# Summing v over each partition's keys before the expert guess, and a new order of GpSimd's work in batches 0 and 1

## The chip, the cores and the metric

The kernel runs on one core of one Trainium2 chip. The metric is the device time of one execution in microseconds (us). Five engines of the core work side by side, each through its own instruction list in order: TensorE (PE in the profile; PEld is its weight load), VectorE (DVE), ScalarE (ACT), GpSimd (POOL) and SyncE (SP, which here only issues transfers). They wait for each other through semaphores. Transfers are issued by SP, ACT or POOL and run on 16 shared DMA engines.

## What is computed

Grouped-query attention, then a mixture of experts, for 8 batches of 384 tokens:

```python
B, Hq, S, D = 8, 16, 384, 64          # 4 key/value heads, 4 query heads each
scores = q @ k.T / sqrt(D)            # softmax over the keys, per head
attn   = exp(scores) / sum(exp(scores))
x      = (attn @ v) as (B*S, 1024)    # all heads of a token side by side
g_idx  = argmax(x @ w_group)          # one of 4 groups, per token
e_idx  = argmax(x @ w_expert[g_idx])  # one of 4 experts of that group
h      = relu(x @ w1[g_idx, e_idx])   # 1024 x 1024
out    = p_group * p_expert * (h @ w2[g_idx, e_idx])
```

p_group and p_expert are the softmax weights of the choices. The scores are small, so attn @ v is close to the mean of v over the keys. With these inputs all 384 tokens of a batch choose the same expert.

## The kernel before, in words

**Batches and units.** The attention of a batch is cut into 24 units u: 4 key/value heads (groups g = u // 6) of 6 pieces of 64 keys. `Attn.run` does for each unit, two units ahead, the scores (L310, TensorE) and their exp (L316, ScalarE, into a tile `e` of a ring of 13), then the products with v (`pv`, L329), then `tail`: GpSimd adds pairs of `e` tiles (L336, emitted at pieces 1 and 3), VectorE reduces four tiles of each group over the partitions' 32-blocks (L343). After a group the sums of products are copied out of PSUM into `xT` (L379 VectorE or L381 ScalarE).

**Softmax sums.** `collect` (L405) adds a group's four reductions on VectorE, `sums` (L415, TensorE, then a reciprocal, L419) finishes them, `spread` (L426, VectorE) spreads the reciprocals over the lanes and `scale_x` (L435) multiplies `xT` by them; `normalise` is the last two on VectorE. `cast` (L244, L246) writes the bf16 copy `xb` that the experts read.

**Guess and fetch.** The weights of one expert are 4 MB. They are fetched before the tokens' own choice is known, for a guessed expert: `guess_mean` (L461) sums v over the keys on TensorE, with slices of v as the stationary side and a column of ones as the moving side (12 products of one column for a batch), `mean_copy` brings the result to SBUF, `guess_logits` (L474) multiplies it by the gate matrix `wgd` (4 products), VectorE picks the largest logit (`first_pick`, `gate_softmax`, `pick_index`), and GpSimd reads the index (`pick`) and issues the fetches of w1 (`pick_w1`, L545) and w2 (`pick_w2`, L551). Ahead of them GpSimd runs a tiny copy (`transposed`, L674) that waits until the next batch's q has been transposed, so that the fetch does not run beside DMA transposes. Experts that were not guessed right are done by a loop at the end (L892); its count is found at run time.

**Order of the work.** All instruction orders are written out by hand (`manual_schedule`). `run` takes a table from unit to inserted steps. Batch 0 (L713) and the first 16 units of batch 1 (L734) hold the first guess, the first fetches, the normalising of batch 0 and the loads of batch 2. Reductions of batch 1 are held back and let go together at unit 11 (`release`). The experts' first product of batch 0, `moe_h(0, 0)` (L607), follows unit 15. From batch 2 on, `block(b)` follows the attention of batch b: `prefetch`, then the experts' products of batch b-1 (`moe_h` L607, `moe_y` L618, output L643/L645/L647) with the softmax sums, the gate logits (L451) and the guess of batch b+1 between them. Batch 7 has no next batch, so its block has no guess. At the end the experts of batch 7 run alone (L879), their outputs are scaled on ScalarE (L884) and VectorE (L882) in turn, and leave by transfers issued on SP, the very last half on ACT (L887).

The start (`first_scores`) casts and transposes the first k and q on TensorE, with `fill` products of ones between, which keep TensorE busy while data arrive.

Of the kernel before, what the change touches and what calls it, by code (L numbers as in the profile page):

```python
# [9 lines left out]
F32 = mybir.dt.float32  # L10
BF16 = mybir.dt.bfloat16
I32 = mybir.dt.int32
AX = mybir.AxisListType
ALU = mybir.AluOpType
# [4 lines left out]
def kernel(  # L19
# [11 lines left out]
    nc = tc.nc  # L31
    P = 128
# [158 lines left out]
    half32 = cpool.tile([P, 2, H2], F32)  # L191
    nc.vector.memset(half32, 0.0)
    wgs = gpool.tile([P, Hkv, NW], F32, name="wgs")
    wgd = cpool.tile([P, Hkv, NW], BF16)
    eidx = cpool.tile([P, NE], F32)
    eback = cpool.tile([P, NE], F32)
    pidx = cpool.tile([P, 3, B, NE], F32)
# [36 lines left out]
    def gate_matrix_b():  # L234
        p2 = ps_tile("x")[:, 1, :Hkv * NW].rearrange("p (g n) -> p g n", n=NW)
        nc.tensor.matmul(out=p2, lhsT=mod64.rearrange("p a m -> p (a m)"), rhs=wgs,
                         start=True, stop=True)
        nc.vector.tensor_copy(out=wgd, in_=p2)

    def evac(eng, out_, in_):
        if eng is nc.scalar:
            eng.copy(out=out_, in_=in_)  # L244
        else:
            eng.tensor_copy(out=out_, in_=in_)  # L246
# [18 lines left out]
    def first_scores():  # L265
        new_kT(0)
        new_qT(0)
        warm = ps_tile("o")

        def fill(n):  # L270
            for i in range(n):
                nc.tensor.matmul(out=warm[:, i % 2, :], lhsT=onesb[:, :P], rhs=onesb, start=True,
                                 stop=True)

        for i in range(4):
            nc.tensor.matmul(out=warm[:, i % 2, :P], lhsT=ones1, rhs=ones1, start=True, stop=True)
        fill(6)
        nc.vector.tensor_copy(out=k16[0][:, :NC].rearrange("p c d -> p (c d)"), in_=k0f[:, 0])
        nc.scalar.copy(out=qraw[0][:, 0], in_=q0f[:, 0])
        nc.vector.tensor_copy(out=qraw[0][:, 1], in_=q0f[:, 1])  # L280
        first_k(0, "s", nc.scalar)
        first_q(0, SC, "s", nc.vector)
        fill(1)
        first_q(SC, SC, "o", nc.vector)
        fill(2)

# [7 lines left out]
    class Attn:  # L294
# [62 lines left out]
        def tail(self, u):  # L357
            b = self.b
            g, c = u // NC, u % NC
            z = u - c  # L360
            if c in (1, 3):
                self.add(nc.gpsimd, u - 1)
            if (b, g) == (2, 0):
                for n in ((), (1,), (2, 0))[max(c, 3) - 3]:
                    self.reduce(g, n, (z, z + 4, z + 5)[n])
            elif c >= 3:
                self.reduce(g, c - 3, (z, z + 4, z + 5)[c - 3])
            if c == NC - 1:
                self.reduce(g, NR - 1, z + 2)
                if b not in xT:  # L370
                    if b == 1:
                        w = wpool.tile([P, KQ, F], BF16, name="w1")
                        xT[b] = w.rearrange("p a f -> p (a f)").bitcast(F32)[
                            :, :KQ * S].rearrange("p (a n) -> p a n", n=S)
                    else:
                        xT[b] = xpool.tile([P, KQ, S], F32, name="xT", bufs=1)
                dst, src = xT[b][:, KG * g:KG * (g + 1), :], self.oT[g][:, :, :S]
                if b > 1 and g < Hkv - 1 or (b, g) == (1, 1):
                    nc.vector.tensor_copy(out=dst, in_=src)  # L379
                else:  # L380
                    nc.scalar.copy(out=dst, in_=src)  # L381
# [64 lines left out]
    def gate_logits(b, pt):  # L446

        for kq in range(KQ):
            x = xT[b][:, kq, :].rearrange("p (c t i) -> p t c i", t=4, i=32)
            for t in range(4):  # L450
                nc.tensor.matmul(out=pt[32 * t:32 * t + 32, 0, :32 * SC], lhsT=wg[:, kq, :],  # L451
                                 rhs=x[:, t], start=(kq == 0), stop=(kq == KQ - 1))

    def guess_mean(b, pt):

        pm = pt[:, 1, :Hkv]
        v16 = vraw[b].rearrange("p h x -> p (h x)").bitcast(BF16)
        for g in range(Hkv):
            for i in range(SC):
                e0 = g * NC * D + i * P  # L460
                nc.tensor.matmul(out=pm[:, g:g + 1], lhsT=v16[:, 2 * e0 + 1:2 * (e0 + P):2],  # L461
                                 rhs=onesb[:, :1], start=(i == 0), stop=(i == SC - 1))

    def mean_copy(pt, eng):
        vm = gpool.tile([P, Hkv], BF16, name="vm")
        evac(eng, vm, pt[:, 1, :Hkv])
        return vm

    def guess_row(pt):
        return pt[:, 1, 64:64 + NW]  # L470

    def guess_logits(vm, pt):
        for g in range(Hkv):
            nc.tensor.matmul(out=guess_row(pt), lhsT=vm[:, g:g + 1].to_broadcast([P, P]),  # L474
                             rhs=wgd[:, g, :], start=(g == 0), stop=(g == Hkv - 1))

    def gate_softmax(b, pt, guess):

# [104 lines left out]
    def out_weights(b):  # L583
        m = gpool.tile([P, SC, NE], F32, name="m")
        nc.vector.tensor_tensor(out=m, in0=cw_all[:, b],
                                in1=oh1_all[:, b, :].unsqueeze(1).to_broadcast([P, SC, NE]),
                                op=ALU.mult)
        we = gpool.tile([P, SC], F32, name="we", bufs=2)
        nc.vector.tensor_reduce(out=we, in_=m, axis=AX.X, op=ALU.add)
        weff[b] = we  # L590
# [43 lines left out]
    def moe_h(b, f0, which, mid=None):  # L634
        if f0 == 0:
            hTs[b] = xpool.tile([P, FQ, S], BF16, name="hT", bufs=1)
        ffn_h(xb[b], w1s[b], hTs[b], f0, which, mid)
# [14 lines left out]
    def do(f, *a):  # L652
        return lambda: f(*a)
# [54 lines left out]
    def first_spread():  # L708
        state["rb"] = spread(0, 1)

    GB = KG * SC
    a = at[0]
    a.run(0, NU, {  # L713
        1: [do(first_q, GB, GB, "x", nc.vector)],
        3: [cast_k],
        4: [gate_matrix_b],
        6: [do(collect, 0, 0, 1)],
        7: [do(first_q, 2 * GB, 2 * GB, "x", nc.vector)],
        8: [do(first_k, 1, "x", nc.vector)],
# [1 line left out]
        13: [first_guess],  # L721
        14: [do(cast, 0, 0)],
        15: [do(collect, 0, 1, 2), first_pick],
        16: [first_fetch],
        19: [do(sums, 0, 1, 2, "x")],
        20: [first_spread],
        21: [first_scale],
    }, at[1])
# [3 lines left out]
    a = at[1]  # L732
    hold(a)
    a.run(0, FU, {  # L734
        3: [do(pick_w2, 0)],
        4: [do(sums, 0, 2, Hkv, "x")],
        6: [do(normalise, 0, 2, "x"), do(normalise, 0, 3, "x")],
        9: [do(load_k, 2), do(load_q, 2)],
        10: [do(cast, 0, 2)],
        11: [a.release, do(collect, 1, 0, 2)],  # L740
        13: [do(cast, 0, 3)],
    })
    moe_h(0, 0, "s")
    load_v(2, nc.gpsimd)
# [10 lines left out]
    weights[0] = gate_softmax(0, pt, True)  # L755
    pick_index(1)
    moe_h(0, 6, "s")
    a.run(FU, NU, {})

    def first_block():  # L760

# [39 lines left out]
    def block(b):  # L801
        last = b == B - 1
        f = b - 1
        if not last:
            prefetch(b)
        moe_h(f, 0, "s")
        collect(b, 0, Hkv)
        weights[f]()
        out_weights(f)
        moe_h(f, 2, "s")  # L810
        sums(b, 0, Hkv, "o")
        for m in range(4):
            normalise(b, m)
        moe_h(f, 4, "s")
        moe_h(f, 6, "s")
        cast(b, 0)
        cast(b, 1)
        moe_y(f, 0, "s")
        cast(b, 2)
        cast(b, 3)  # L820
        y = ffn_y(w2s[f], hTs[f], 1, "s", (0,))
        pt = ps_tile("o")
        gate_logits(b, pt)
        if not last:
            guess_mean(b + 1, pt)
            vm = mean_copy(pt, nc.vector)
        ffn_y(w2s[f], hTs[f], 1, "s", (1,), y)
        y_out(f, 1, y)
        if not last:
            guess_logits(vm, pt)  # L830
        weights[b] = gate_softmax(b, pt, not last)
        y = ffn_y(w2s[f], hTs[f], 2, "o", (0,))
        if not last:
            pick_index(b + 1)
            at[b + 1] = Attn(b + 1)
            y_scores(f, at[b + 1], y)
            return {}
        ffn_y(w2s[f], hTs[f], 2, "o", (1,), y)
        y_out(f, 2, y, nc.vector)
        weights[b]()  # L840
        out_weights(b)
# [28 lines left out]
    for c in range(SC):  # L870
        ot = opool.tile([P, DM], F32, name="ot")
        w = weff[B - 1][:, c:c + 1]
        parts = [(0, HALF), (HALF, DM)]
        if c == SC - 1:
            parts = [(0, HALF), (HALF, 3 * HALF // 2), (3 * HALF // 2, DM)]
        for i, (n0, n1) in enumerate(parts):
            y = ps_tile("so"[i % 2])
            for f in range(FQ):
                nc.tensor.matmul(out=y[:, 0, :n1 - n0], lhsT=hTs[B - 1][:, f, c * P:(c + 1) * P],  # L879
                                 rhs=w2s[B - 1][:, f, n0:n1], start=(f == 0), stop=(f == FQ - 1))  # L880
            if i % 2:
                nc.vector.tensor_scalar(ot[:, n0:n1], y[:, 0, :n1 - n0], w, None, op0=ALU.mult)  # L882
            else:
                nc.scalar.mul(ot[:, n0:n1], y[:, 0, :n1 - n0], w)  # L884
            for j, (ps, x) in enumerate(halves(c)):
                eng = nc.scalar if j and n1 - n0 < HALF and i == 2 else nc.sync
                eng.dma_start(out=out_rows(out[(B - 1) * S:])[x][:, n0:n1], in_=ot[ps, n0:n1])  # L887
    region.close()

# [84 lines left out]
```

## Time and profile before

| | us |
|---|---|
| four runs | 367.66 to 369.09, median 367.97 |
| the profiled execution | 367.97 |
| its span, first to last instruction | 366.3 |
| end of its last matmul | 359.3 |
| TensorE / VectorE / ScalarE / GpSimd busy | 354.5 / 258.9 / 229.0 / 152.2 |
| attention of batch 3, units 0 to 23 | 124.0 to 143.1 |
| experts' block between two attentions | 100.0 to 124.0 |
| after the last attention | 315.3 to 366.3 |

The profiled execution's own time equals the median of the runs; 1.6 us of it lie outside its span. "Busy" counts an instruction from its start to its end; matmuls overlap each other, so a busy TensorE can still have its instructions further apart or closer together. The chain of waits follows the execution back from its last instruction, at each step to what released it. A line number names the line of the kernel; where a helper records an operation it is the helper's.

### The profile page before, as it was taken

The page shows a single profiled execution, that of the slowest core. Times are in us where ns is not written, and L with a number is a line of the kernel's source. Part 1 is how long each engine was busy: PE and PEld are TensorE (multiplying, and loading weights), DVE is VectorE, ACT ScalarE, POOL GpSimd, SP SyncE. Part 2 cuts the span into 40 slices and gives each one's busy share as a digit, 9 for nine tenths or more (in the row PEclk, how much of TensorE's full clock was granted, in tenths as well). Part 3 has the DMA queues.
Part 4 walks back from the last instruction along what each step waited for, and adds up shares of the span by engine and source line. Part 5 has one row for each costly group of instructions (what it writes and reads, how often), then busy time and mean ns, then how long its engine had stood idle before and what let it go on. Part 6 is the DMA issues. An engine that isn't in the chain of part 4 may idle for free.

```text
span 366.3 us, 9583 instructions
## 1 busy us (share of the span) xinstructions
PE 354.5 (97%) x3989; PEld 185.8 (51%) x4004; DVE 258.9 (71%) x500; ACT 229.0 (63%) x300; POOL 152.2 (42%) x120
## 2 busy tenths in 40 slices
PE   8999899999999999999999999999999999999992
PEld 4554465455455445554455555554555545555641
DVE  5698799759975698837878479755997459892130
ACT  5799835659835796348944498356963579444221
POOL 6756960517704375035732177042760258300000
PEclk9999999999999999999999999999999999999998
DMA  8976999899999999899999999999997699997234
GB/s 189 252 115 105 192 207 197 177 229 244 209 138 196 257 238 207 143 215 268 222 152 185 196 265 210 143 205 240 240 208 128 96 272 229 214 212 179 70 86 92
DMA packets 69903, 69.81 MB, mean 191 GB/s; under 512 B 35832, under 2 KB 49944, under 8 KB 69856
## 3 DMA queue, kind: packets, MB, share of 16 engines
q0 software_dynamic: 26864, 41.81, 65.0%
q1 hardware_dynamic: 42560, 26.80, 31.9%
q8 instruction: 33, 0.54, 0.6%
q10 hardware_dynamic: 432, 0.54, 0.5%
q14 instruction: 14, 0.11, 0.1%
HBM read 89.21 MB, written 12.58 MB: 278 GB/s over the span
## 4 chain that ended last, share of the span: by engine, by line
PE 90%; DVE 3%; ACT 2%; DMA 1%; issue 1%; POOL 1%; ACTq 0%
PE ps_o L329 30%; PE ps_s L607 22%; PE ps_s L618 13%; PE ps_s L310 8%; PE ps_o L618 7%; PE ps_o L451 3%; PE ps_s L879 2%; DVE red L343 1%; PE ps_o L607 1%; PE ps_o L879 1%; ACT e L316 1%; PE ps_o L415 1%; DMA w<-in_q_dram 1%; PE ps_o L461 1%; DVE ps_o L426 1%
## 5 line engine op out<-in xcount | busy, mean ns | idle before, releaser
L316 ACT ACTIVATE e<-ps_s 128x768 f32<-128x768 f32 x192 | 150.1, 815 | 19.2 <-PE ps_s L310 16.5
L329 PE MATMUL ps_o<-e,v_raw 64*64 64x384 f32 x1536 | 153.1, 482 | 0.2 <-DVE xT L435 0.2
L336 POOL TENSOR_TENSOR e<-e 128x768 f32<-128x768 f32 x64 | 116.0, 1831 | 80.1 <-ACT e L316 59.3
L343 DVE TRANSPOSE_TENSOR_REDUCE red<-e 128x24 f32<-128x768 f32 x128 | 114.1, 946 | 18.4 <-POOL e L336 18.3
L607 PE MATMUL ps_s<-xb,w 128*128 128x384 bf16 x480 | 81.0, 326 | 0.1
L329 PEld LDWEIGHTS ps_o<-e,v_raw 64*64 64x64 f32 x1536 | 55.6, 133 | 37.4 <-issue 27.0
L607 PEld LDWEIGHTS <-w 128*128 128x128 bf16 x512 | 48.9, 98 | 35.8 <-issue 4.2
L310 PE MATMUL ps_s<-qT,kT 64*64 64x384 bf16 x768 | 63.7, 326 | 0.5 <-ACT e L316 0.2
L611 ACT ACTIVATE hT<-ps_s 128x768 bf16<-128x768 f32 x30 | 24.3, 811 | 61.0 <-PE ps_s L607 61.0
L618 PE MATMUL ps_s<-w,hT 128*128 128x512 bf16 x211 | 49.0, 379 | 0.9 <-issue 0.2
L618 PEld LDWEIGHTS <-hT 128*128 128x128 bf16 x336 | 31.3, 98 | 36.6 <-issue 2.1
L310 PEld LDWEIGHTS <-kT 64*64 64x64 bf16 x768 | 24.5, 105 | 38.4 <-issue 36.5
L643 ACT ACTIVATE ot<-ps_s,we 128x1024 f32<-128x1024 f32 x14 | 15.6, 1115 | 27.3 <-PE ps_s L618 27.3
L674 POOL COPY after<-qT 128x1 bf16<-128x1 bf16 x7 | 2.4, 344 | 69.7 <-DMA qT<-q_raw 66.0
L426 DVE STREAM_TRANSPOSE rb<-inv 128x384 f32<-128x384 f32 x60 | 31.0, 554 | 0.3
L618 PE MATMUL ps_o<-w,hT 128*128 128x512 bf16 x111 | 26.3, 379 | 0.1
L435 DVE TENSOR_TENSOR xT<-xT,rb 128x768 f32<-128x768 f32 x25 | 24.0, 958 | 0.9
L244 ACT CAST xb<-xT 128x768 bf16<-128x768 f32 x27 | 21.1, 828 | 0.0
L379 DVE COPY xT<-ps_o 128x768 f32<-128x768 f32 x18 | 16.5, 919 | 0.0
L246 DVE CAST vm<-ps_o 128x4 bf16<-128x4 f32 x6 | 1.0, 162 | 21.0 <-PE ps_o L461 21.0
L645 DVE TENSOR_SCALAR ot<-ps_o,we 128x1024 f32<-128x1024 f32 x7 | 9.0, 1282 | 5.6 <-PE ps_o L618 5.1
L545 POOL DMA_DIRECT2D w<-in_moe_w_dram x8 | 7.3, 915 | 12.4 <-PE ps_s L310 9.7
(125 smaller groups left out, 197.2 us busy)
## 6 DMA issues: line engine op xcount, KB each, us to landing
w<-in_moe_w_dram POOLq DMA_DIRECT2D x16, 2048.0 KB, 23.2
out_dram<-ot SPq DMA_DIRECT2D x42, 256.0 KB, 6.8
q_raw<-in_q_dram POOLq DMA_DIRECT2D x7, 768.0 KB, 31.4
v_raw<-in_v_dram SPq DMA_DIRECT2D x12, 384.0 KB, 5.5
k<-in_k_dram POOLq DMA_DIRECT2D x7, 192.0 KB, 28.1
out_dram<-ot SPq DMA_DIRECT2D x10, 128.0 KB, 2.3
v_raw<-in_v_dram POOLq DMA_DIRECT2D x2, 384.0 KB, 12.2
w<-in_q_dram POOLq DMA_DIRECT2D x3, 192.0 KB, 6.7
```

The costliest lines, as they stand in the source:

```text
L244: eng.copy(out=out_, in_=in_)
L310: nc.tensor.matmul(out=sT[r * H2:(r + 1) * H2, s, :S], lhsT=kT[b][s * D:(s + 1) * D, slot, ks], rhs=qT[b][s * D:(s + 1) * D, kq * SC:(kq + ...
L316: nc.scalar.activation(e.rearrange("p t (s x) -> p s t x", s=2), sT[:, :, :S].rearrange("p s (t x) -> p s t x", t=2), ACT.Exp, scale=scale)
L329: nc.tensor.matmul(out=oT[t * D:(t + 1) * D, r, :S], lhsT=vraw[b][r * H2:(r + 1) * H2, g, c * D:(c + 1) * D], rhs=self.e[u][r * H2:(r + 1) ...
L336: eng.tensor_add(out=self.e[u], in0=self.e[u], in1=self.e[u + 1])
L343: nc.vector.tensor_reduce(out=reds[self.b][:, g, n].rearrange("p t j -> p (t j)"), in_=self.e[u].rearrange("p t (j x) -> p (t j) x", x=32) ...
L379: nc.vector.tensor_copy(out=dst, in_=src)
L426: nc.vector.transpose(out=rb[:, r].rearrange("p (j x) -> p j x", x=32), in_=inv[b][:, 2 * m + r].unsqueeze(2).to_broadcast([P, NB, 32]))
L435: eng.tensor_mul(out=x, in0=x, in1=rb)
L607: nc.tensor.matmul(out=h[:, jj, :S], lhsT=w1[:, kq, (f0 + jj) * P:(f0 + jj + 1) * P], rhs=x[:, kq, :], start=(kq == 0), stop=(kq == KQ - 1))
L611: nc.scalar.activation(hT[:, f0:f0 + 2, :], h[:, :, :S], ACT.Relu)
L618: nc.tensor.matmul(out=y[:, nh, :], lhsT=hT[:, f, c * P:(c + 1) * P], rhs=w2[:, f, nh * HALF:(nh + 1) * HALF], start=(f == 0), stop=(f == ...
```

## The change

1. **The sum of v.** A new step `sum_v` adds, on every partition, the 6 keys that lie there, for 4 heads of 64 columns (1536 numbers to 256, fp32 in, bf16 out). For batches 1 and 3 to 7 it is one VectorE reduce; for batches 0 and 2 it is three adds on GpSimd (768, 256 and 256 wide). `guess_mean` then needs 2 products of one column instead of 12, with two heads side by side, and `guess_logits` 2 instead of 4; `wgd` is laid out for two heads side by side, which takes two copies of half the partitions instead of one.
2. **Where `sum_v` stands.** Batch 0: GpSimd, after unit 4 of batch 0, behind `cast_k`. Batch 1: VectorE, after unit 5 of batch 1. Batch 2: GpSimd, after unit 21 of batch 1. Batches 3 to 7: VectorE, in the block before, between `out_weights` and the second `moe_h`.
3. **First fetch.** `first_fetch` moves from unit 16 to unit 19 of batch 0, so GpSimd's add of unit 19 stands ahead of it.
4. **Group 2 of batch 0** is scaled on GpSimd (`second_scale`, after unit 5 of batch 1) and no longer on VectorE after unit 6; the add of unit 3 of batch 1 and the fetch of w2 (unit 3 before) stand right behind it. The casts of groups 2 and 3 move from units 10 and 13 to units 9 and 11.
5. **Start and end.** One `fill` product between the first transposes goes. In the last outputs the second half of every part that ScalarE scales is issued by ACT, not by SP: three transfers more on ACT, three fewer on SP.

```diff
-    wgd = cpool.tile([P, Hkv, NW], BF16)
+    wgd = cpool.tile([P, Hkv // 2, NW], BF16)
...
-        nc.vector.tensor_copy(out=wgd, in_=p2)
+        for r in range(2):
+            nc.vector.tensor_copy(out=wgd[r * H2:(r + 1) * H2], in_=p2[r * H2:(r + 1) * H2, r::2])
...
         first_q(0, SC, "s", nc.vector)
-        fill(1)
         first_q(SC, SC, "o", nc.vector)
...
-            if c in (1, 3):
+            if c in (1, 3) and (b, u) != (1, 3):
                 self.add(nc.gpsimd, u - 1)
...
+    def sum_v(b, eng):
+        vsum[b] = gpool.tile([P, Hkv, D], BF16, name="vsum")
+        with nc.allow_low_precision("only serves a guess"):
+            if eng is nc.vector:
+                eng.tensor_reduce(out=vsum[b], in_=vraw[b].rearrange("p g (c d) -> p g d c", d=D),
+                                  axis=AX.X, op=ALU.add)
+                return
+            n = NC // 2 * D
+            t = gpool.tile([P, 2, S], F32, name="rb", bufs=2).rearrange(
+                "p a s -> p (a s)").rearrange("p (g n) -> p g n", g=Hkv)
+            eng.tensor_add(out=t, in0=vraw[b][:, :, :n], in1=vraw[b][:, :, n:])
+            eng.tensor_add(out=t[:, :, :D], in0=t[:, :, :D], in1=t[:, :, D:2 * D])
+            eng.tensor_add(out=vsum[b], in0=t[:, :, :D], in1=t[:, :, 2 * D:])
...
     def guess_mean(b, pt):
-        pm = pt[:, 1, :Hkv]
-        v16 = vraw[b].rearrange("p h x -> p (h x)").bitcast(BF16)
-        for g in range(Hkv):
-            for i in range(SC):
-                e0 = g * NC * D + i * P
-                nc.tensor.matmul(out=pm[:, g:g + 1], lhsT=v16[:, 2 * e0 + 1:2 * (e0 + P):2],
-                                 rhs=onesb[:, :1], start=(i == 0), stop=(i == SC - 1))
+        for j in range(Hkv // 2):
+            nc.tensor.matmul(out=pt[:, 1, j:j + 1],
+                             lhsT=vsum[b][:, 2 * j:2 * j + 2, :].rearrange("p g d -> p (g d)"),
+                             rhs=onesb[:, :1], start=True, stop=True)
...
     def guess_logits(vm, pt):
-        for g in range(Hkv):
-            nc.tensor.matmul(out=guess_row(pt), lhsT=vm[:, g:g + 1].to_broadcast([P, P]),
-                             rhs=wgd[:, g, :], start=(g == 0), stop=(g == Hkv - 1))
+        n = Hkv // 2
+        for j in range(n):
+            nc.tensor.matmul(out=guess_row(pt), lhsT=vm[:, j:j + 1].to_broadcast([P, P]),
+                             rhs=wgd[:, j, :], start=(j == 0), stop=(j == n - 1))
...
+    def second_scale():
+        scale_x(0, 2, spread(0, 2), nc.gpsimd)
...
-        4: [gate_matrix_b],
+        4: [gate_matrix_b, do(sum_v, 0, nc.gpsimd)],
...
-        16: [first_fetch],
-        19: [do(sums, 0, 1, 2, "x")],
+        19: [first_fetch, do(sums, 0, 1, 2, "x")],
...
-        3: [do(pick_w2, 0)],
         4: [do(sums, 0, 2, Hkv, "x")],
-        6: [do(normalise, 0, 2, "x"), do(normalise, 0, 3, "x")],
-        9: [do(load_k, 2), do(load_q, 2)],
-        10: [do(cast, 0, 2)],
-        11: [a.release, do(collect, 1, 0, 2)],
-        13: [do(cast, 0, 3)],
+        5: [second_scale, do(a.add, nc.gpsimd, 2), do(pick_w2, 0), do(sum_v, 1, nc.vector)],
+        6: [do(normalise, 0, 3, "x")],
+        9: [do(load_k, 2), do(load_q, 2), do(cast, 0, 2)],
+        11: [a.release, do(collect, 1, 0, 2), do(cast, 0, 3)],
...
-    a.run(FU, NU, {})
+    a.run(FU, NU, {21: [do(sum_v, 2, nc.gpsimd)]})
...
         out_weights(f)
+        if not last:
+            sum_v(b + 1, nc.vector)
         moe_h(f, 2, "s")
...
-                eng = nc.scalar if j and n1 - n0 < HALF and i == 2 else nc.sync
+                eng = nc.scalar if j and i % 2 == 0 else nc.sync
```

More of the change, by code (lines that the diff above doesn't have):

```diff
@@ L452, in gate_logits @@
                                  rhs=x[:, t], start=(kq == 0), stop=(kq == KQ - 1))
-    def guess_mean(b, pt):
-        pm = pt[:, 1, :Hkv]
-        v16 = vraw[b].rearrange("p h x -> p (h x)").bitcast(BF16)
-        for g in range(Hkv):
-            for i in range(SC):
-                e0 = g * NC * D + i * P
-                nc.tensor.matmul(out=pm[:, g:g + 1], lhsT=v16[:, 2 * e0 + 1:2 * (e0 + P):2],
-                                 rhs=onesb[:, :1], start=(i == 0), stop=(i == SC - 1))
+    vsum = {}
+    def sum_v(b, eng):
[11 more added lines that the diff above has]
+            eng.tensor_add(out=vsum[b], in0=t[:, :, :D], in1=t[:, :, 2 * D:])
+    def guess_mean(b, pt):
+        for j in range(Hkv // 2):
+            nc.tensor.matmul(out=pt[:, 1, j:j + 1],
+                             lhsT=vsum[b][:, 2 * j:2 * j + 2, :].rearrange("p g d -> p (g d)"),
+                             rhs=onesb[:, :1], start=True, stop=True)
     def mean_copy(pt, eng):
-        vm = gpool.tile([P, Hkv], BF16, name="vm")
-        evac(eng, vm, pt[:, 1, :Hkv])
+        vm = gpool.tile([P, Hkv // 2], BF16, name="vm")
+        evac(eng, vm, pt[:, 1, :Hkv // 2])
         return vm
```

## The prediction

> **What bounds the kernel.** I read the first line of the page first.
>
> ```profile
> PE 354.5 (97%) x3989; PEld 185.8 (51%) x4004; DVE 258.9 (71%) x500; ACT 229.0 (63%) x300; POOL 152.2 (42%) x120
> ```
>
> TensorE is busy for 97% of the span, so an edit counts where it takes work from TensorE, or where TensorE waits. The clock granted to it is full until 362 us, so no stage runs slower than another for that reason. The chain of waits then shows where the edited steps lie. Here it is in the block of batch 3 (start, length, what; xN counts instructions):
>
> ```profile
> 116.25 1.46 PE ps_o L451 x64
> 117.70 0.39 PE ps_o L461 x12
> 118.09 0.08 issue
> 118.17 1.67 PE ps_s L618 x7
> 119.84 0.09 PE ps_o L474 x4
> ```
>
> The guess (L461, L474) stands between other TensorE work, nothing else is waited for, and the end is set through it. The same stretch of batch 7, which has no guess, goes straight from L451 to L618:
>
> ```profile
> 331.45 1.46 PE ps_o L451 x64
> 332.91 0.16 issue
> 333.07 1.67 PE ps_s L618 x7
> ```
>
> From L451's end to L618 it is 0.47 us with the guess and 0.16 without. In batches 0 and 1 the chain leaves TensorE:
>
> ```profile
> 31.40 1.83 POOL e L336
> ...
> 33.26 3.57 DVE red L343 x4
> ...
> 36.85 0.49 DVE rsum L405
> ...
> 37.38 0.42 PE ps_o L415 x8
> ...
> 46.81 0.82 ACT e L316
> ...
> 47.67 2.76 PE ps_s L607 x16
> ```
>
> GpSimd's last add of batch 0 stands behind the first fetch; VectorE, the softmax sums, ScalarE's exps and the first experts' product follow from it.
>
> **1. Guess products: -2.1 us.** In the trace the weight loads of L461 start 0.025 us apart, and so do those of L474. Ten pairs fewer (12 to 2) and two fewer (4 to 2) make 12 x 0.025 = 0.30 us per batch, which agrees with the 0.31 just read. Eight guesses: those of batch 1 (51.9), batch 2 (78) and batches 3 to 7 (blocks as above) lie on the chain: 7 x 0.30 = 2.1. Batch 0's (22.65, 24.78) lies in a stretch where ScalarE works without a break from 20.5 to 36.5 and the next thing waited for is VectorE at 37.38; I count it 0 (ends 0 and 0.3).
>
> The Trainium skill, "TensorE: Matmul & The Clock Gate", section "Back-to-back issue gap", gives about 81 ns for a sustained pair of load and product at 128 columns, and some 25 ns as the issue floor for narrow ones. By the first figure, 84 pairs would be worth an estimated 6.8 us; the trace shows 25 ns with a one-column moving side and 128-column weights, and the trace decides.
>
> **2. VectorE's reduce: 0, if it is short enough.** No row shows a reduce with a 256-byte stride. The nearest:
>
> ```profile
> L405 DVE TENSOR_REDUCE rsum<-red 128x96 f32<-128x384 f32 x6 | 4.8, 807 | 0.2
> L866 DVE TENSOR_REDUCE left<-pkey 128x1 f32<-128x128 f32 x1 | 0.3, 288 | 0.0
> L497 DVE TENSOR_REDUCE el<-pr 128x16 f32<-128x64 f32 x7 | 1.9, 266 | 0.2
> L525 DVE TENSOR_REDUCE fmx<-ps_o 128x1 f32<-128x4 f32 x1 | 0.2, 155 | 0.0
> ```
>
> With 0.15 us fixed (L525, 4 elements), L866 gives (288-150)/128 = 1.08 ns per element in order and L405, whose four addends lie apart, (807-150)/384 = 1.71. For 1536 elements that is 1.8 to 2.8 us. I take 2.8, since L405 too reads apart. In a block it stands behind these:
>
> ```profile
> 104.88 0.20 DVE L589 TENSOR_REDUCE we<-m 128x3 f32<-128x48 f32 x1
> 105.81 0.76 DVE L419 RECIPROCAL inv<-ps_o 128x96 f32<-128x96 f32 x1 [0.72 <-PE ps_o L415]
> ...
> 113.49 0.96 DVE L435 TENSOR_TENSOR xT<-xT,rb 128x768 f32<-128x768 f32 x1
> 118.13 0.16 DVE L246 CAST vm<-ps_o 128x4 bf16<-128x4 f32 x1 [3.68 <-PE ps_o L461]
> ```
>
> The 0.72 us idle ahead of L419 takes its start; the other 2.1 are queued in front of L419, the transposes (L426) and the scalings (L435), whose last then ends at 114.45 + 2.1 = 116.5. Its readers: the last quarter of L451, from 117.15 on, and ScalarE's casts of xb, up to 0.2 us late, with no ScalarE work due until 119.9. So it costs nothing; VectorE's 3.68 us of idle pay. With a reduce of over about 3.4 us the cover is gone, and each further us costs one in each of five blocks.
>
> **3. The stretch of batches 0 and 1: -0.1 us.** GpSimd, step by step. Its three adds of v follow `cast_k` (ends 13.70): 768 wide, 1.83 by the rows of L336; 256 wide, a third, some 0.65 each; so they end near 16.95. The adds of units 7 and 9 (15.06 and 17.57 before) then end at 18.8 and 20.6, and VectorE's reduction that stands at 18.54 starts near 18.85; about 0.4 us of that (ends 0 and 0.9) passes through VectorE to `spread(0, 1)`, which ends at 32.3 instead of 31.9. The add of unit 19 has its operands at 27.4 and now stands ahead of the fetch:
>
> ```profile
> 29.82 0.19 POOL L674 COPY after<-qT 128x1 bf16<-128x1 bf16 x1 [3.74 <-DVE red L343]
> 30.45 0.93 POOL L545 DMA_DIRECT2D w<-in_moe_w_dram  x1 [0.44 <-issue]
> ```
>
> It fits into the 3.74 us idle (done 29.3). The wait that the tiny copy makes ends at 29.8 as before, so the fetch of w1 is not moved (it lands 13.9 us later at 44.4, needed at 47.6). VectorE no longer waits 1.36 us for GpSimd: four reductions 32.3 to 35.9, L405 to 36.4, and L415 starts near 36.45 instead of 37.38: 0.9 us earlier.
>
> But GpSimd then has this: the add of unit 21 (ends 33.2), the scaling of group 1 (1.81, 35.0), the cast (0.82, 35.85), the add of unit 1 of batch 1 (37.65); then it waits for `spread(0, 2)`, which follows L415 by 0.92 (sums, reciprocal) and 1.04 (two transposes): 38.45. The new scaling (1.81 by L435 on GpSimd) ends at 40.3, the add of unit 3 at 42.1, the fetch of w2 (0.94) at 43.05, and the adds of units 7 and 9 at 46.65; before, 45.73. The order of waits of the changed program makes the exp of unit 16 reuse the buffer that the add of unit 9 reads last: 46.65 + 0.81 is 47.5, and L607 waits for that exp: 47.55 against 47.67. So of the 0.9 only 0.1 is left (ends -0.3 and +0.4, from the shift of 0 to 0.9 and the unknown short adds). Moved with it and covered: w2 is fetched 1 us later (lands about 57, needed 67.4); k and q of batch 2 are issued at 46.7 for 45.7, their transposes end near 72 for 71, needed at 79; the second w1 follows that at 72.7 and 18.6 us later is still ahead of 100. The cast of group 2 finds its scaling done (40.3, ScalarE there at 41.5). VectorE's `sum_v(1)` (38.5 to 41.25) puts the last scaling to 43.45, where TensorE's products of unit 12 are ready near 43. GpSimd's sum for batch 2 (67.4 to 70.6, v landed by 65) ends before the next fetch's wait.
>
> **4. The tail: -0.64 us.** SP issues its last five transfers at 358.20, 358.71, 359.40, 359.99 and 360.69, without a gap, while the last ScalarE scaling ends at 359.71: the last issue is 1 us behind its data. With the one of 358.71 on ACT (0.54, in an idle stretch up to 359.23), the last starts 0.59 + 0.05 = 0.64 earlier. This page line shows the SP queue's share (0.595 median, the last 1.55):
>
> ```profile
> L887 SPq DMA_DIRECT2D out_dram<-ot x13: 466/595/1548, 351.8 to 360.7; - x13
> L887 ACTq DMA_DIRECT2D out_dram<-ot x1: 541/541/541, 359.7 to 359.7; - x1
> ```
>
> Ends: 0 (if the landing sets the end anyway) and 1.6 (if the long last issue shrinks to the median too).
>
> **5. The rest: 0.** The `fill` product that goes lies in a wait of TensorE for VectorE until 5.86; if it was the cover of anything, 0.1. The second copy of `wgd` (0.2 on VectorE at 13.2) falls into 0.98 us idle before 16.49.
>
> **Sum:** 2.1 + 0 + 0.1 + 0.64 + 0 = 2.84; 367.97 - 2.84 = 365.1. The profiled execution equals the median of the runs, so nothing is shifted. Least gain 2.1 - 0.3 + 0 = 1.8 (366.2), most 2.4 + 0.4 + 1.6 = 4.4 (363.6).
>
> **Rivals.** *GpSimd becomes the bound earlier* (chance 0.14): some adds take longer (a pair at 22.03 takes 4.05 where others take 3.6), or the short adds cost more than a third. The adds that end at 46.65 have no slack left, so each us passes one to one to L607; 1.4 more gives 366.5, the bound 366.9. For it: three adds, a scaling and a wait are added to GpSimd there. Against: GpSimd is idle 2.64 us before 22.03 and 3.74 before 29.82, which absorbs the first part.
>
> *The wait on GpSimd's add does not end last* (0.13): then ScalarE, 0.9 earlier throughout, sets L607 at 46.75, and the sum is 2.1 + 0.9 + 0.64: 364.3. For it: the four buffers between may free in time if the adds have slack that I do not see. Against: the wait is in the program.
>
> *The strided reduce outlasts its cover* (0.08), the case of a slower kernel. At 3.97 us (2.5 ns per element) five blocks lose 2.85 and the gain is gone; from 4.2 us it is slower by more than 0.3%; at 5 us, 8 - 2.84 = 5.2 lost: 373. For it: no row has such a stride. Against: L405 and L497 read apart as well, at 1.7 to 1.8 ns.
>
> *The change does not do what it says* (0.01): a rounded sum of v guesses another expert, and the loop at the end runs for a batch, some 43 us (one period between attentions, 124 to 100 plus 19): about 410. Against: it is fp32 up to one rounding, and v went in cut to bf16 before.
>
> **How the numbers follow.** Forecast 0.64 (363.6 to 366.2). The range reaches to 366.9 for the first rival; the second lies in it; the 0.09 of the last two stay out. About 0.3% (1.1 us) is what a measurement of this kernel can tell from no change: faster by more than that are the forecast, the second rival and 0.06 of the first (0.83); within it, 0.08 of the first; slower, 0.09.
>
> **What would show it.** In the profile after: 16 guess products of each kind in all; 0.16 to 0.22 us between L451 and the next experts' product in the blocks, and no wait ahead of L451; the reduce's own duration (2.8) with the last scaling near 116.5 less what was gained; L415 of batch 0 near 36.4, GpSimd's adds done near 46.6 and the first experts' product at 47.5 behind an exp that waited for GpSimd; the fetch of w1 still at 30.4; SP's last issue 0.64 closer to the last matmul. A TensorE wait for VectorE in front of L451, or a fetch of w1 that moved, would make the prediction wrong.

## The result, and the profile after

The changed kernel takes 367.1 us (median of 52 runs, 366.17 to 370.22); the kernel before, 368.04 in the same comparison (median of 77). The ratio is 0.9976, 95% interval [0.9969, 0.9984]: 0.9 us faster. The interval leaves out 1, but the difference is less than the 0.3% (1.1 us) that the prediction took as what can be told from no change. The forecast was 365.1, range 363.6 to 366.9. The profiled execution of the changed kernel took 366.52, 0.6 below its median; the one of before stood at its median. The positions below are those of the two profiled executions.

| | before | after | difference | forecast |
|---|---|---|---|---|
| start to the first experts' product (L607, now L622) | 47.67 | 49.03 | +1.36 | -0.1 |
| from there to TensorE's last piece of the chain | 311.54 | 309.43 | -2.11 | -2.1 |
| from there to the end of the span | 7.1 | 6.4 | -0.7 | -0.64 |
| sum | 366.3 | 364.9 | -1.45 | -2.84 |

Two of the three stretches came as forecast. The first line of the page shows TensorE's work 1.9 us shorter and 97 products fewer, and VectorE 16.7 us busier, six sums of 2.8:

```profile
PE 352.6 (97%) x3892; PEld 183.1 (50%) x3907; DVE 275.6 (76%) x506; ACT 229.9 (63%) x300; POOL 160.3 (44%) x127
```

The chain of waits of the changed kernel, in the block of batch 3 (start, length, what), has the guess at 0.14 and 0.04 instead of 0.39 and 0.09:

```profile
117.00 1.46 PE ps_o L451 x64
118.46 0.14 PE ps_o L474 x2
...
118.67 1.67 PE ps_s L633 x7
120.35 0.04 PE ps_o L489 x2
```

No wait stands ahead of L451. VectorE's instructions there, by the timeline:

```profile
105.76 2.81 DVE L461 TENSOR_REDUCE vsum<-v_raw 128x256 bf16<-128x1536 f32 x1
...
116.17 0.96 DVE L435 TENSOR_TENSOR xT<-xT,rb 128x768 f32<-128x768 f32 x1
118.64 0.16 DVE L247 CAST vm<-ps_o 128x2 bf16<-128x2 f32 x1 [1.51 <-PE ps_o L474]
```

The sum takes 2.81 us (2.8 forecast, 1.83 ns per element), the last scaling ends at 117.13, about 0.8 ahead of the last quarter of L451 (117.95), and the idle time in front of L247 shrank from 3.68 to 1.51.

The loss is in batch 0. VectorE's and then GpSimd's timeline of the changed kernel, around the add of unit 19:

```profile
27.94 1.72 DVE L580 TENSOR_SCALAR oh_all<-key,km 128x16 f32<-128x16 f32 x1
29.69 0.18 DVE L583 SCALAR_TENSOR_TENSOR t<-eidx,oh_all 128x16 f32<-128x16 f32 x1
```

```profile
27.80 1.82 POOL L336 TENSOR_TENSOR e<-e 128x768 f32<-128x768 f32 x1 [1.16 <-ACT e L316]
31.02 0.19 POOL L689 COPY after<-qT 128x1 bf16<-128x1 bf16 x1 [1.39 <-DVE red L343]
```

L580 is a comparison of 16 numbers. Before, as L565, it took 0.23 us:

```profile
27.39 0.23 DVE L565 TENSOR_SCALAR oh_all<-key,km 128x16 f32<-128x16 f32 x1
```

Now it starts 0.14 behind GpSimd's add and ends 0.04 behind it: it stood for 1.5 us. The index that it belongs to is ready at 30.06 instead of 28.03, GpSimd is idle for 1.39 us until it has it, and VectorE's reductions behind it are as late. The sums of batch 0 (L415) then start at 37.94, where the forecast had 36.45, and GpSimd waits for VectorE's spread of group 2 before its new scaling, which the forecast had at 38.45:

```profile
40.02 1.83 POOL L435 TENSOR_TENSOR xT<-xT,rb 128x768 f32<-128x768 f32 x1 [1.15 <-DVE rb L426]
```

From there GpSimd works without a gap (scaling, add, fetch of w2) until 44.51; ScalarE's exps, which also follow L415, reach the next add's operand at the same 44.51, and the profile's chain goes through them up to there. From 44.5 on the chain in front of the first experts' product is GpSimd's, and its adds end 2.4 us later than before (48.15 for 45.73) and 1.5 later than forecast (46.65):

```profile
44.52 1.34 POOL e L336
...
46.32 1.83 POOL e L336
...
48.17 0.82 ACT e L316
```

### The profile page after: what moved, and what is told of

The parts are those of the page before. It is cut to its first block, busy times and chain, and to the rows that moved or that the text cites. A ratio compares the mean times of both kernels' runs of the same rounds, so it can differ in the third digit from the quotient of the medians.

```text
span 364.9 us, 9409 instructions
## 1 busy us (share of the span) xinstructions
PE 352.6 (97%) x3892; PEld 183.1 (50%) x3907; DVE 275.6 (76%) x506; ACT 229.9 (63%) x300; POOL 160.3 (44%) x127
## 4 chain that ended last, share of the span: by engine, by line
PE 85%; DVE 5%; POOL 3%; ACT 2%; issue 1%; DMA 1%; ACTq 0%; POOLq 0%
PE ps_o L329 27%; PE ps_s L622 22%; PE ps_s L633 13%; PE ps_s L310 7%; PE ps_o L633 7%; PE ps_o L451 3%; DVE red L343 3%; POOL e L336 2%; PE ps_s L896 2%; ACT e L316 1%; PE ps_o L622 1%; DMA w<-in_moe_w_expert_dram 1%; PE ps_o L896 1%; PE ps_o L415 1%; DVE rb L426 1%
## 5 line engine op out<-in xcount | busy, mean ns | idle before, releaser
L622 PE MATMUL ps_s<-xb,w 128*128 128x384 bf16 x480 | 81.0, 326 | 0.5 <-ACT e L316 0.5
L622 PEld LDWEIGHTS <-w 128*128 128x128 bf16 x512 | 48.8, 98 | 36.2 <-issue 4.7
L426 DVE STREAM_TRANSPOSE rb<-inv 128x384 f32<-128x384 f32 x62 | 32.0, 554 | 0.4
L435 DVE TENSOR_TENSOR xT<-xT,rb 128x768 f32<-128x768 f32 x25 | 24.0, 958 | 0.9
L461 DVE TENSOR_REDUCE vsum<-v_raw 128x256 bf16<-128x1536 f32 x6 | 16.9, 2811 | 0.0
L381 ACT COPY xT<-ps_o 128x768 f32<-128x768 f32 x10 | 8.0, 804 | 6.6 <-PE ps_o L329 6.6
```

The lines of the kernel that those rows point to most:

```text
L426: nc.vector.transpose(out=rb[:, r].rearrange("p (j x) -> p j x", x=32), in_=inv[b][:, 2 * m + r].unsqueeze(2).to_broadcast([P, NB, 32]))
L435: eng.tensor_mul(out=x, in0=x, in1=rb)
L461: eng.tensor_reduce(out=vsum[b], in_=vraw[b].rearrange("p g (c d) -> p g d c", d=D), axis=AX.X, op=ALU.add)
L622: nc.tensor.matmul(out=h[:, jj, :S], lhsT=w1[:, kq, (f0 + jj) * P:(f0 + jj + 1) * P], rhs=x[:, kq, :], start=(kq == 0), stop=(kq == KQ - 1))
```

## The experiments

**Theory A**: the stall of VectorE's comparison beside the add of unit 19, which the change put there, is the loss. **Rival B**: GpSimd's added work (three adds, a scaling) is the loss by itself. "Product at" is the start of the first experts' product in the profiled execution. "Behind the cast" measures from `cast_k`, since the start of the kernel varies: 34.49 before, 35.67 after. Ratios are to the kernel before.

| kernel | product at | behind the cast | median us | ratio, 95% interval |
|---|---|---|---|---|
| early_deferred | 47.96 | 34.00 | 365.5 | 0.9935 [0.9915, 0.9955] |
| pure_stall | 47.41 | 34.03 | 365.47 | 0.9941 [0.9923, 0.9960] |
| early_beside | 53.67 | 38.72 | 366.75 | 0.9962 [0.9946, 0.9979] |
| fetch_first | 48.76 | 34.85 | 366.5 | 0.9961 [0.9945, 0.9976] |
| mean_on_tensor | 47.34 | 33.91 | 365.14 | 0.9930 [0.9910, 0.9950] |
| index_later | 48.61 | 35.05 | 366.5 | 0.9949 [0.9927, 0.9972] |
| vector_scale | 49.53 | 36.21 | 367.19 | 0.9968 [0.9949, 0.9988] |
| sum_only | 49.24 | 35.26 | 366.84 | 0.9960 [0.9938, 0.9982] |
| fill_back | 49.16 | 35.58 | 367.05 | 0.9964 [0.9945, 0.9983] |
| tail_only | 47.42 | 34.25 | 367.5 | 0.9996 [0.9974, 1.0018] |
| double_sum | 48.84 | 35.77 | 378.99 | 1.0265 [1.0216, 1.0313] |
| late_w2 | 46.74 | 33.59 | 365.22 | 0.9925 [0.9907, 0.9944] |
| late_w2_mean | 46.27 | 33.03 | 364.99 | 0.9920 [0.9903, 0.9936] |

**early_deferred.** The index of batch 0 without the comparison:

```diff
+        nc.vector.scalar_tensor_tensor(key, oh_first, -float(NE), eid16, op0=ALU.mult, op1=ALU.add)
+        nc.vector.tensor_reduce(out=e_i, in_=key, axis=AX.X, op=ALU.min)
...
-        pick_index(0)
+        early_index()
...
+        first_one_hot()
         out_weights(0)
```

> The changed kernel, but for batch 0 the guessed index comes from two VectorE instructions (key, minimum) that end before GpSimd's add of unit 19 starts, and the one-hot row (the instruction that took 1.72 us) is made later, in the block. Theory A (VectorE's stall beside GpSimd's add of unit 19 is the loss): no VectorE instruction of 1.7 us there; fetch of w1 issued near 31.15 (31.65), L415 of batch 0 near 36.2 (37.94), first experts' product near 47.45 (49.03), time 1.5 us under the changed kernel: 365.6. Rival B (GpSimd's added work, three adds and a scaling, is the loss by itself): first experts' product stays at or after 48.6, time 366.7 to 367.1.

Measured: 365.5, product 34.00 behind the cast (1.67 sooner than in the changed kernel). In absolute time the product stands at 47.96, 0.5 over theory A's 47.45, but the cast of k was 0.6 later here. The time is A's (365.6) and not B's (366.7 to 367.1), although the three adds and the scaling were still on GpSimd.

**pure_stall.** The same, with about as much VectorE work as was taken out, in a form that reads one tensor:

```diff
         early_index()
+        for _ in range(3):
+            pad = gpool.tile([P, 1], F32, name="km")
+            nc.vector.tensor_reduce(out=pad, in_=eid16, axis=AX.X, op=ALU.max)
```

> The kernel of early_deferred, with three small reduces of one SBUF tensor (0.6 us together) on VectorE where the moved instructions stood, so that VectorE has as much work there as in the changed kernel, but nothing that GpSimd's add stops. It separates the stall from the shorter list. Theory A: first experts' product 34.1 behind the cast of k (early_deferred 34.00, changed kernel 35.67), time 365.6. Rival (part of the gain came from the instructions taken out): 34.6 and 366.1.

Measured: 34.03 and 365.47. VectorE's and GpSimd's timelines:

```profile
27.86 0.57 DVE L718 TENSOR_REDUCE km<-eid 128x1 f32<-128x16 f32 x3
```

```profile
27.74 1.83 POOL L338 TENSOR_TENSOR e<-e 128x768 f32<-128x768 f32 x1 [1.07 <-ACT e L318]
```

The three reduces ran beside the same add of GpSimd (27.74 to 29.57), unhindered. So it is the stall, not the length of the list.

**early_beside.** The early index, with the one-hot row made right behind it:

```diff
-        pick_index(0)
+        early_index()
+        first_one_hot()
```

> The changed kernel with the same early index, but the one-hot row is made right behind it, so that VectorE still stands beside GpSimd's add of unit 19. It tells the late fetch from the late VectorE. Theory A in the form that VectorE's delay counts (it reaches GpSimd through the spread of group 2): fetch of w1 near 31.15, VectorE's instruction behind the index stalled to 29.6, spread of group 2 still done near 40, first experts' product near 49.1, time as the changed kernel, 367.1. The form in which the late fetch counts: first experts' product near 48.5, time 366.6.

Measured: 366.75, between the two expectations, so the time does not decide. Its profiled execution is an odd one (371.1 us), but shows the way of the delay: there VectorE was stopped twice, first in an instruction of 1.62 us beside the add of unit 19, then, by the timeline,

```profile
31.40 2.60 DVE L587 TENSOR_SCALAR oh_all<-key,km 128x16 f32<-128x16 f32 x1
```

behind GpSimd's issue of the fetch (31.19 to 32.11) and the add after it (to 33.96). The fetch of w1 was early, and GpSimd still waited for VectorE (its scaling of group 1 began at 37.95, after 3.99 us of idle that VectorE's spread ended). TensorE, too, waited 3.04 us for VectorE there, until 36.85, and from 38.0 to 41.4 the clock granted to it was 0.50. That is of the size by which this execution exceeds the median, 4.4 us, but no second execution of this run was profiled. The delay travels through VectorE's spreads, not through the fetch.

**fetch_first.** Part 3 undone: the fetch ahead of the add again.

```diff
+        16: [first_fetch],
-        19: [first_fetch, do(sums, 0, 1, 2, "x")],
+        19: [do(sums, 0, 1, 2, "x")],
```

> The changed kernel with the first fetch back at unit 16, ahead of GpSimd's add of unit 19 (part 3 undone alone). Theory A: no stall of VectorE in the index (GpSimd is idle then), fetch of w1 at 30.45, L415 at 37.4 behind the late add as before the change, first experts' product near 48.55, time 0.5 under the changed kernel: 366.6. Rival B (GpSimd's own work bounds): first experts' product at 49.0 or later, since the add is later by 3.6 us; 367.1 to 367.6.

Measured: 366.5. L580 takes 0.23 again (28.48), the late add holds VectorE up instead, as before the change. In absolute time the product stands at 48.76, as the cast of k was 0.56 later than in the changed kernel; behind the cast it is 0.82 sooner, 0.3 more than expected.

**mean_on_tensor.** The other ingredient: batch 0 sums on TensorE again (`first_mean`, the 12 products of before), and the add of unit 19 stays ahead of the fetch.

```diff
-        4: [gate_matrix_b, do(sum_v, 0, nc.gpsimd)],
+        4: [gate_matrix_b],
...
-        guess_mean(0, state["pt"])
+        first_mean(state["pt"])
```

> The changed kernel, but batch 0 sums its keys by the 12 products on TensorE, as before the change, so GpSimd has no adds of v behind the cast of k. Theory A: a late cast of k is taken up by idle time again, VectorE's index comes 0.55 earlier, but GpSimd's add of unit 19 starts at 27.6 all the same, and the next instruction of the index with two SBUF inputs or one that copies (at 27.66) is stopped to 29.5: the stall moves to another instruction, the first experts' product comes at 48.6 to 48.8 in absolute time, 366.7. If the index passes just ahead of the add: no stall, product at 47.4, 365.3. If the three adds are the loss rather than the stall: no more than 0.2 above the second, with the stall in the profile.

Measured: 365.14, product at 47.34: the second of the three cases. VectorE's and GpSimd's timelines:

```profile
27.37 0.23 DVE L582 TENSOR_SCALAR oh_all<-key,km 128x16 f32<-128x16 f32 x1
27.64 0.17 DVE L585 SCALAR_TENSOR_TENSOR t<-eidx,oh_all 128x16 f32<-128x16 f32 x1
...
27.86 0.15 DVE L588 CAST e_i<-ef 128x1 int32<-128x1 f32 x1
```

```profile
27.68 1.82 POOL L338 TENSOR_TENSOR e<-e 128x768 f32<-128x768 f32 x1 [1.61 <-ACT e L318]
```

The comparison is over, and L585 began 0.04 us ahead of the add; the conversion of one number behind it ran beside the add in 0.15.

**index_later.** If it is a race, harmless work ahead of the index must lose it:

```diff
         first_choice(guess_row(state["pt"]))
+        for _ in range(3):
+            pad = gpool.tile([P, 1], F32, name="km")
+            nc.vector.tensor_reduce(out=pad, in_=eback, axis=AX.X, op=ALU.max)
         pick_index(0)
```

> The kernel of mean_on_tensor (no stall: the index's last instruction with two SBUF inputs started 0.04 us ahead of GpSimd's add of unit 19) with three small reduces of one SBUF tensor (0.6 us) put ahead of the index. If the loss is a matter of which of the two engines starts first: the comparison L580 now starts behind the add, takes 1.5 to 1.7 us instead of 0.23, the index comes 2.0 later for 0.6 us of work, first experts' product at 48.7 to 49.1 (47.34), time 366.6. If the index is only late by the work put ahead of it: product at 47.4 to 47.9, 365.2 to 365.7.

Measured: 366.5, product at 48.61, 1.27 later for 0.6 us of reduces (0.1 short of what was expected; GpSimd's add, too, came 0.3 earlier in this execution). The comparison and the add in its timelines:

```profile
27.45 1.79 DVE L582 TENSOR_SCALAR oh_all<-key,km 128x16 f32<-128x16 f32 x1
```

```profile
27.39 1.82 POOL L338 TENSOR_TENSOR e<-e 128x768 f32<-128x768 f32 x1 [1.61 <-ACT e L318]
```

It started 0.06 behind the add and stood until the add's end. In these rows the one that starts first runs through, and the other waits for its end.

**vector_scale** undoes part 4, **sum_only** parts 3 and 4 together:

```diff
-        5: [second_scale, do(a.add, nc.gpsimd, 2), do(pick_w2, 0), do(sum_v, 1, nc.vector)],
-        6: [do(normalise, 0, 3, "x")],
+        3: [do(pick_w2, 0)],
+        5: [do(sum_v, 1, nc.vector)],
+        6: [do(normalise, 0, 2, "x"), do(normalise, 0, 3, "x")],
```

> The changed kernel with part 4 undone: group 2 is scaled on VectorE again (behind the sum of v of batch 1), the fetch of w2 and the casts stand where they stood. Theory A: VectorE's stall stays (the same instruction takes 1.7 us), but it no longer reaches GpSimd's adds through the wait for the spread of group 2; these end near 45.3, and ScalarE's casts, that now wait for VectorE (scaling done 46.0), set the first experts' product: 47.8 (34.45 behind the cast of k, changed kernel 35.67), time 1.2 under the changed kernel: 365.9. Rival (VectorE's delay costs the same by whatever way): product at 48.9, 367.0.

> Parts 1, 2 and 5 alone: the sums of v stand where the change puts them, the first fetch and group 2 are as before. Theory A: no stall of VectorE at the index, L415 of batch 0 behind the late add as before, VectorE's sum of v of batch 1 hidden; first experts' product 34.5 behind the cast of k (before 34.49), then the 2.1 of the guess products and 0.6 of the tail come through in full: 365.3. Rival (GpSimd's three adds and VectorE's sum cost by themselves): product at 35.3 or later, 366.1 and more.

Both missed. Measured 367.19 (product 36.21 behind the cast, 34.45 expected) and 366.84 (35.26, 34.5 expected). The chain of sum_only, in front of its first experts' product at 49.24:

```profile
46.61 1.75 DVE red L343 x2
...
48.37 0.82 ACT e L316
```

The exp of unit 16 also waits for two VectorE reductions of batch 1, and these stand behind VectorE's sum of v of batch 1 (2.83 us, 38.55 to 41.38) and both scalings. I had looked at the casts and not at these reductions, though the kernel before has them on its chain too (45.05, ahead of the exp at 46.81). So the sum of batch 1 is not hidden by itself: without part 4 the product comes 0.8 later behind the cast than before. Part 4 takes the scaling of group 2 off VectorE (0.95 us) and puts its spread ahead of the sum, which makes room for it. The rival of sum_only (product at 35.3 or later) has the right size; that GpSimd's adds have a part in it is not shown.

**fill_back** puts the fill product of the start back, **tail_only** gives the kernel before the transfers of part 5:

```diff
         first_q(0, SC, "s", nc.vector)
+        fill(1)
         first_q(SC, SC, "o", nc.vector)
```

```diff
-                eng = nc.scalar if j and n1 - n0 < HALF and i == 2 else nc.sync
+                eng = nc.scalar if j and i % 2 == 0 else nc.sync
```

> The changed kernel with the one fill product put back. Question: the profiled executions with and without the change reach GpSimd's cast of k (the last thing at the start) at 13.2 before and 13.4 to 15.0 after. If the missing fill product makes the start later: cast of k near 13.2, time 0.5 under the changed kernel, 366.6. Rival (the start varies from execution to execution whatever the kernel, and the change only takes away the idle time of GpSimd behind the cast that took it up): time as the changed kernel, 367.1.

> The kernel before, with part 5's transfers on ACT alone. Prediction's term: SP's last issue starts 0.64 earlier, span and time 0.64 shorter, 367.4. Rival: the landing or the end of the program sets the end, time within 0.2 of before, 367.9. From the two profiled executions the end came 0.7 sooner behind the last product, which speaks for the first; the medians moved 0.5 less than the profiled executions, which leaves room for the second.

fill_back: 367.05, no difference; the cast of k stood at 13.59, waiting, by the timeline, for a transfer:

```profile
13.59 0.51 POOL L289 CAST w<-w 128x384 bf16<-128x384 f32 x1 [0.35 <-DMA w<-in_k_dram]
```

Nine of the thirteen profiled executions with the change show this wait, up to 0.9 us; the two without it show none. With the fill product back the wait is still there, so its absence is not the cause; two executions are too few to say that the change is. tail_only: 367.5, 0.45 less, with an interval that holds 1: not settled by time. From the last product to the end of its span it took 6.86 us (7.13 before); of the thirteen profiled executions that have part 5 with the rest, eleven took 6.4 to 6.6, and two 7.0 and 7.3. The issue on SP does begin 0.6 sooner behind the last product (0.88 for 1.50 us) and takes 0.55 for 1.55, but the engines then wait longer for the last landing, so the shorter issue, the upper end of the tail's range, does not come through.

**double_sum** writes the sum of v twice in the five blocks:

```diff
             sum_v(b + 1, nc.vector)
+            sum_v(b + 1, nc.vector)
```

> The changed kernel with VectorE's sum of v done twice in the five blocks (the second writes the same numbers). It tests the cover of the prediction: one sum of 2.81 us ends the last scaling 0.9 us ahead of the last quarter of L451, so the second pushes it 1.9 us past: each of five blocks 1.9 longer, time 9.5 over the changed kernel: 376.6. If the cover is larger than read (no wait of TensorE there): 367.1.

Measured: 378.99, 11.9 over the changed kernel (9.5 expected). The cover ends about where it was read. The chain of the first of the blocks:

```profile
118.80 0.97 DVE xT L435
...
119.82 0.54 PE ps_o L451 x16
```

The last quarter of L451 waits for the last scaling, and each block is 2.09 us longer (1.9 expected). In the profiled execution 1.7 us more came after the fifth block's wait: the 18 experts' products behind it took 5.7 us, 4.1 in the first block. The windows, whose last columns are granted clock, share of the transfers and GB/s, show the clock halved there:

```profile
300.00:303.00 3.00, 3.00 (x10) 1.08 (x9) 0.02 (x1) 0.00 (x0) 0.00 (x0) 0.50 1.07 214
```

**late_w2** and **late_w2_mean** look for a better order: early_deferred with the fetch of w2 behind GpSimd's adds, and the same with batch 0's sum on TensorE.

```diff
-        5: [second_scale, do(a.add, nc.gpsimd, 2), do(pick_w2, 0), do(sum_v, 1, nc.vector)],
+        5: [second_scale, do(a.add, nc.gpsimd, 2), do(sum_v, 1, nc.vector)],
...
-        9: [do(load_k, 2), do(load_q, 2), do(cast, 0, 2)],
+        9: [do(pick_w2, 0), do(load_k, 2), do(load_q, 2), do(cast, 0, 2)],
```

> The kernel of early_deferred with GpSimd's fetch of w2 behind its adds of units 7 and 9 of batch 1 instead of ahead of them. From its profile: GpSimd's add then ends 0.94 earlier, VectorE's reductions (46.4) set the exp of unit 16, first experts' product 33.4 behind the cast of k (34.00), time 0.6 under early_deferred: 364.9. w2 lands near 61 and is needed at 67. Rival (something else is as late): 365.5.

> Late w2, early index and batch 0's sum on TensorE together. If the late cast of k costs through GpSimd's adds of v: first experts' product at 46.7 to 47.0 in absolute time whenever the cast comes, 364.4. If it does not: as late_w2, 364.9.

Measured: 365.22 and 364.99. The products come 0.4 and 1.0 sooner behind the cast than in early_deferred. For late_w2 that is 33.59 where 33.4 was expected, but its time lies between the expectation (364.9) and the rival (365.5) and decides nothing. late_w2_mean has its product sooner than expected (46.27) and yet the time of the case in which the cast does not matter (364.9); in it nothing is waited for in front of it but TensorE and ScalarE. The times lie within each other's intervals and that of early_deferred, but late_w2_mean is 2.9 us under the kernel before (367.9 in the same comparison) and 2.1 under the changed one.

## Why the prediction was wrong

The step that failed is in part 3: "It fits into the 3.74 us idle (done 29.3)". It does fit into GpSimd's idle time. I asked what is queued behind the add on GpSimd, and not what VectorE does in those 1.8 us. It ran the index of the guess there, and one of its instructions could not run beside the add. The line "VectorE no longer waits 1.36 us for GpSimd" stayed true, and 1.5 us of another wait for the same engine took its place: L415 at 37.94 for the 36.45 forecast, the first experts' product at 49.03 for 47.55. pure_stall shows its price: 1.6 us of time by the medians (367.1 to 365.47), 1.3 by the ratios to the kernel before, with about the same amount of VectorE work.

The second half of the failure is the "about 0.4 us" by which GpSimd's three adds push VectorE; it was 0.55, and I valued it as 0.4 us of delay. It decides a race: with the adds of v, the comparison starts 0.14 behind GpSimd's add; without them (mean_on_tensor), the index gets past it by 0.04. Either ingredient taken away takes the stall away: the moved add in fetch_first, which gives back 0.8 behind the cast, the adds of v in mean_on_tensor, which gives back 1.7 in absolute time.

The sign was in the trace of before, in VectorE's and GpSimd's timelines:

```profile
21.67 0.96 DVE L435 TENSOR_TENSOR xT<-xT,rb 128x768 f32<-128x768 f32 x1
```

```profile
22.03 4.05 POOL L336 TENSOR_TENSOR e<-e 128x768 f32<-128x768 f32 x2 [2.64 <-PE ps_s L310]
```

The pair of adds that I quoted for the first rival took 4.05 us and not 3.6 because its first one took 2.27: it was issued while VectorE's L435, with two inputs in SBUF, ran (to 22.62). I read it as an add that takes longer beside other work; but it ended 1.68 us behind L435's end, near the 1.82 of an add with nothing in its way, as if it had waited. After the change the same pair shows it again: L435 ran from 22.21 to 23.17, and the add issued at 22.21 took 2.64 and ended 1.68 us behind it, too.

The Trainium skill, "SBUF — State Buffer", section "Who interferes with whom", describes this: VectorE and GpSimd share a pair of ports, held for a whole instruction by whichever starts first; against GpSimd's reads stand VectorE instructions with two SBUF inputs, and copies, casts and `tensor_scalar` instructions in their two-port modes, but not `tensor_reduce`. The runs agree with it: 1.5 us for a comparison of 16 numbers (a `tensor_scalar`), none for three reduces. Whether L580 was in such a mode no trace shows.

Point by point:

- **Guess products, -2.1**: right, -2.11, and no batch's share was hidden.
- **VectorE's reduce, 0**: right in duration (2.81) and cover in the blocks; double_sum shows where the cover ends.
- **Batches 0 and 1, -0.1**: wrong, +1.36. The adds were priced rightly (1.83 and twice 0.73, estimated 0.65), and the fetch of w1, which I named as what would make the prediction wrong if it moved, did move, from 30.45 to 31.65: not for its transposes but for the index. The wait of the exp on GpSimd's add, taken from the order of waits, was the one that ended last, as forecast.
- **The first rival** (GpSimd's adds end late) came true in its place and price, 1.5 us late, but not for its reason. Some adds were slower than forecast (0.73 for 0.65, and 4.42 for the pair at 22.21), but GpSimd was idle for 1.16 us behind them, ahead of the add of unit 19.
- **The tail, -0.64**: -0.7 between these two executions, -0.27 for tail_only; about the size, not settled to better than 0.4.
- **The rest, 0**: fill_back finds no difference (367.05 for 367.1).
- **The strided reduce and the guess that picks another expert**: neither happened.

What stays open is half a us: the two profiled executions differ by 1.45, the medians by 0.94. Two things could make up the rest. The tail varies from execution to execution, and the cast of k, late by up to 1.6 us, had 1.36 us of GpSimd's idle time behind it before the change and the adds of v now. No run takes these apart.

## What to carry to other kernels

Before an instruction is moved into an engine's idle time, list what the other engines run in that stretch: VectorE and GpSimd can stop each other for a whole instruction, and the short one pays for the long one. Where a moved instruction starts within a fraction of a us of such a neighbour, a small shift elsewhere is worth the whole instruction, so give both orders a price. Small steps that only serve a guess are best built from forms that do not stop (here a reduce in place of a comparison).

## What was not expected of the hardware

- A reduce over a 256-byte stride takes 2.81 us for 1536 numbers per partition, 1.83 ns each; on GpSimd the same sum takes 3.3 (1.83 + 0.73 + 0.73).
- A comparison of 16 numbers took 2.60 us behind GpSimd's issue of a fetch and the add after it (early_beside).
- After waits of TensorE (0.28 and 1.40 us) in the fifth block of double_sum, the granted clock was 0.50 for some 3 us (300 to 303) and 0.93 in the next 3, which cost 1.7 us; the four earlier blocks waited as long and lost nothing of the kind. In early_beside it was 0.50 from 38.0 to 41.4, after a wait of 3.04. What decides it is not shown.
